# One list of work in two orders: linear attention with memory beside a dense layer, on one Trainium2 core

## The chip, the cores and the metric

The kernel runs on one core of one Trainium2 chip. A core has a matrix engine (PE in the profile, with PEld for its weight loads), a vector engine (DVE), a scalar engine (ACT), a general engine (POOL), a queue processor (SP) and 16 DMA engines. Each engine takes its own instructions strictly in order; engines meet only through semaphores. The metric is device time in microseconds of one execution; smaller is better. Time before: 229.43 us, the median of three runs (228.73 to 229.71).

## What is computed

One layer norm feeds two branches, and the input is added to their sum.

```python
def _A_ref(x, wq, wk, wv, wo, beta):          # S=2048, D=512, H=32 heads of 16, N=4 segments of L=512
    ...
    phi = lambda t: jnp.where(t > 0, t + 1.0, jnp.exp(t))
    g = _sigmoid(beta)
    for s in range(N):
        logits = jnp.einsum('bhqd,bhkd->bhqk', qs, ks) * scale + mask
        a_dot = jnp.einsum('bhqk,bhkd->bhqd', _softmax(logits), vs)
        a_mem = (phi(qs) @ M) / (phi(qs) . z + 1e-06)
        o = g * a_mem + (1.0 - g) * a_dot
        M, z = M + phi(ks)^T vs, z + sum(phi(ks))
    return o @ wo

def _B_ref(x, w1, w2):                        # F=1792
    return _silu(x @ w1) @ w2

xn = _layernorm(A_x)
return A_x + _A_ref(xn, ...) + _B_ref(xn, ...)
```

(The three lines on a_mem, M and z are shortened from einsums of the same meaning.)

## The kernel before

The work is cut into some 1,500 small pieces, each a Python function that issues the instructions of one piece on one engine. The string ORDER, a list written out by hand at the head of the file, names the pieces one after the other; the loop at the end of the kernel walks the list and calls each function. Nothing reorders the instructions after that, so the order of the words is the order on each engine. A word is a kind with numbers: `h0.10.2` is part 2 of block 10 of the first dense product of segment 0.

The kinds that matter here, with their lines:

- `S` (scores, lines 654 to 669): the scores of four heads go through PE into the tile psS, four banks of PSUM, of which there is one buffer; one ACT instruction (line 669) takes the exponential of all 2,048 columns into SBUF, and POOL masks the diagonal (677). There are 80 such pieces. The line of the list that begins with `S17` is called stage S17 below. The order of the 80 stages is the same in both lists.
- `E`, `O` (696): weights times values for the even and odd heads; `Ev`, `Ov`, `Oa` copy them out (v on DVE, a on ACT).
- `k`, `q`, `v`, `h` (322 or 324, in four parts or two): the dense products; `kv`, `qv`, `vv` copy a finished one out of PSUM on DVE, `ka`, `qa`, `va` do it on ACT (361, 371, 378). `ha` is the tanh of h on ACT (457), `hv` the rest of silu on DVE (462).
- `o`, `oc`, `od`, `oh`: the output product in whole, half or quarter width, 18 products of 512 columns for each of 16 row blocks; `st`, `sh` add the input and store (586, 633).
- `fa`, `ga` (395): the exponential of phi on ACT; `fp`, `gp` and `fv`, `gv` are its parts on POOL and DVE. `s`, `r`, `w`, `z`, `d`, `n`, `R`, `W`: sums, reciprocals, weights and their spreading over partitions by DMA.
- The layer norm: `xs` (or `xc`, `xd`) statistics on DVE, `xq` a square root on ACT (289), `xi` a reciprocal, `Nv` the normalised rows, `X` a transpose on PE with its copies `Xa`, `Xv` (743), `XD` a transpose by DMA (749). Rows 0 to 3 of the 16 use `xq`; later groups of four use `xg` on POOL.
- `tb` (295): one tiny exponential on ACT, whose only use is that the table of that function is loaded then. A first tiny square root (193) does the same for the square root at the start, before the list. The built program has a table load on ACT wherever the function changes between the square root and the others.
- `busy` (756): idle products of 128 columns on zeros. `lw0`, `lw1` (176): the loads of w2 and wo, issued from ACT's queue. `xl` (579): the load of a row block of the input, from SP.

A product counts as 512 columns. The four PSUM banks that psS leaves are shared by all other products (the pool `pp`, four buffers); a new product waits until the copy of an old one has run.

## Time and profile before

| | |
|---|---|
| median of the runs | 229.43 us (228.73 to 229.71) |
| span of the profiled execution | 227.4 us |
| what lies around the span, by the median | 2.0 us |
| PE busy | 217.2 us, 96% of the span |
| ACT busy | 198.0 us, 87% |
| DVE busy | 177.7 us, 78% |
| POOL busy | 113.9 us, 50% |
| 80 exponentials of the scores on ACT (669) | 150.2 us, 1,878 ns each |
| 56 tanh on ACT (457) | 32.8 us, 597 ns each (some overlap with what is ahead) |
| granted TensorE clock | 1.000 |

The page gives the time of the profiled execution's span alone; the 2.0 us is the median of the runs less that span. A busy PE is no PE at its peak: the ends of matmuls are modelled, and they overlap. What a stage costs is read from the starts of the exponentials in the timeline of ACT. From the first to the last of them, 12.72 to 206.62 us, there are 79 stages.

### The profile page before, as it was taken

What the parts mean: (1) busy time and instruction counts of PE and PEld (TensorE: products, weight loads), DVE (VectorE), ACT (ScalarE), POOL (GpSimd) and SP (SyncE); (2) the same over time, 40 slices, a digit from 0 to 9 for tenths busy, and PEclk for the clock granted to TensorE, in tenths of its full rate; (3) what the DMA queues carried; (4) which work ended last, traced back from release to release, by engine and by line L of the source; (5) the groups of instructions that cost most, each with busy time, mean ns of one, the idle gap of its engine ahead of it and who ended that gap; (6) DMA issues with size and microseconds to landing.
All of it is one profiled execution on the core that took longest, in us unless ns stands there. A gap on an engine that the chain in (4) does not pass through costs nothing.

```text
span 227.4 us, 7543 instructions
## 1 busy us (share of the span) xinstructions
PE 217.2 (96%) x3124; PEld 112.9 (50%) x3152; DVE 177.7 (78%) x351; ACT 198.0 (87%) x179; POOL 113.9 (50%) x173
## 2 busy tenths in 40 slices
...
ACT  3799998999999999999999899999999989897000
...
GB/s 181 361 381 68 77 52 299 60 55 57 61 22 158 72 35 47 96 15 112 41 40 113 75 53 58 35 117 42 22 100 66 88 36 84 29 63 130 29 90 94
DMA packets 34787, 20.55 MB, mean 90 GB/s; under 512 B 15680, under 2 KB 34240, under 8 KB 34752
## 3 DMA queue, kind: packets, MB, share of 16 engines
...
q8 instruction: 24, 0.39, 0.8%
...
HBM read 9.96 MB, written 2.10 MB: 53 GB/s over the span
## 4 chain that ended last, share of the span: by engine, by line
PE 62%; ACT 11%; DVE 11%; DMA 8%; issue 4%; SPq 2%; POOL 0%; DVEq 0%
PE ps L322 18%; PE psO L322 14%; PE psS L662 9%; ACT Pb L669 8%; PE ps L324 8%; PE psO L324 6%; PE psV L696 6%; DMA x_hi<-in_A_x_dram 4%; DMA spr<-rz 3%; ACT th L457 2%; DMA x_res<-in_A_x_dram 2%; DVE stats L272 1%; DVE o_out L586 1%; DVE kT L361 1%; PE psM L324 1%
## 5 line engine op out<-in xcount | busy, mean ns | idle before, releaser
L669 ACT ACTIVATE Pb<-psS 128x2048 bf16<-128x2048 f32 x80 | 150.2, 1878 | 5.8 <-PE psS L662 5.1
L677 POOL TENSOR_SCALAR_AFFINE_SELECT Pb<-Pb 128x512 bf16<-128x512 bf16 (+1 forms) x112 | 80.1, 729 | 85.1 <-ACT Pb L669 83.7
L462 DVE SCALAR_TENSOR_TENSOR hT<-th,ps 128x512 bf16<-128x512 bf16 x56 | 37.8, 679 | 14.1 <-ACT th L457 13.7
L322 PE MATMUL ps<-xnT,w_sb 128*128 128x512 bf16 (+1 forms) x177 | 43.3, 340 | 0.8 <-issue 0.5
L322 PE MATMUL psO<-w_sb,hT 128*128 128x512 bf16 (+2 forms) x139 | 36.1, 340 | 0.7 <-issue 0.5
L457 ACT ACTIVATE th<-ps 128x512 bf16<-128x512 f32 x56 | 32.8, 597 | 0.5 <-PE ps L322 0.4
L324 PE MATMUL psO<-w_sb,hT 128*32 128x128 bf16 (+2 forms) x468 | 26.7, 300 | 0.0
L322 PEld LDWEIGHTS <-w_sb 128*128 128x128 bf16 x184 | 17.1, 98 | 16.3 <-issue 3.3
L696 PE MATMUL psV<-Pb,Vz 128*32 128x128 bf16 (+3 forms) x512 | 23.1, 300 | 0.4 <-DVE oT L573 0.2
L322 PEld LDWEIGHTS <-hT 128*128 128x128 bf16 x149 | 13.6, 97 | 16.9 <-issue 4.8
L324 PE MATMUL ps<-xnT,w_sb 128*32 128x512 bf16 (+1 forms) x384 | 21.8, 329 | 0.0
L324 PEld LDWEIGHTS <-hT 128*32 128x32 bf16 x636 | 15.7, 97 | 9.7 <-issue 1.7
L696 PEld LDWEIGHTS <-Vz 128*32 128x32 bf16 x512 | 13.0, 96 | 10.6 <-issue 1.4
L662 PE MATMUL psS<-qT,kT 16*128 16x128 bf16 (+3 forms) x256 | 17.3, 301 | 0.9 <-ACT Pb L669 0.8
L662 PE MATMUL psS<-qT,kTo 32*128 32x384 bf16 (+3 forms) x256 | 17.2, 299 | 0.6 <-ACT Pb L669 0.2
L362 POOL TENSOR_SCALAR kTo<-kT,pm_odd 128x512 bf16<-128x512 bf16 x16 | 11.9, 747 | 8.2 <-DVE kT L361 7.3
L322 PE MATMUL ps<-xnT,wk_sb 128*128 128x512 bf16 (+1 forms) x66 | 15.4, 328 | 0.7 <-issue 0.5
L322 PE MATMUL ps<-wv_sb,xnT 128*128 128x512 bf16 x48 | 14.3, 380 | 0.6 <-issue 0.2
L662 PEld LDWEIGHTS <-kT 16*128 16x128 bf16 x256 | 5.9, 91 | 16.7 <-issue 16.2
L361 DVE CAST kT<-ps 128x512 bf16<-128x512 f32 x15 | 10.2, 687 | 4.6 <-PE ps L322 4.3
L586 DVE SCALAR_TENSOR_TENSOR o_out<-psO,x_res 128x512 bf16<-128x512 f32 x14 | 9.6, 687 | 5.3 <-PE psO L322 2.8
L719 DVE CAST oraw<-psV 128x512 bf16<-128x512 f32 x16 | 11.0, 688 | 3.4 <-PE psV L696 3.3
...
## 6 DMA issues: line engine op xcount, KB each, us to landing
...
```

The lines of the kernel that those rows point to most:

```text
L322: return [nc.tensor.matmul(out, lhsT=lhsT, rhs=rhs, start=start, stop=stop, skip_group_check=True)]
L324: nc.tensor.matmul(out[c : c + 32], lhsT=lhsT[:, c : c + 32], rhs=rhs, start=start, stop=stop, tile_position=(0, c), skip_group_check=True,)
L361: copy(out=kT[:, dt, :], in_=sts[s].pop(("k", dt))[:, :])
L362: nc.gpsimd.tensor_scalar(out=kTo[:, dt, :], in0=kT[:, dt, :], scalar1=pm_odd[:, 0:1], scalar2=1.0, op0=ALU.mult, op1=ALU.mult,)
L457: nc.scalar.activation(out=th[:], in_=sts[s]["h", ft][:, :], func=AF.Tanh, scale=0.5)
L462: nc.vector.scalar_tensor_tensor(out=st["hT"][:, ft, :], in0=st.pop(("th", ft))[:], scalar=1.0, in1=st.pop(("h", ft))[:, :], op0=ALU.add, ...
L586: out = nc.vector.scalar_tensor_tensor(out=o_out[:], in0=st.pop(("psO", j)), scalar=0.5, in1=st["x", j][:], op0=ALU.mult, op1=ALU.add)
L662: nc.tensor.matmul(psS[:, g, c0 : c0 + nq], lhsT=kk[rows, dt, kt * P : (kt + 1) * P], rhs=st["qT"][rows, dt, kt * P : L], start=True, stop ...
L669: exp = nc.scalar.activation(out=Pb[:, :, :], in_=psS[:, :, :], func=AF.Exp, scale=SCALE)
L677: mask = nc.gpsimd.affine_select(out=blocks, in_=blocks, compare_op=ALU.is_ge, fill=0.0, base=0, pattern=[[0, blocks.shape[1]], [1, P]], c ...
L696: nc.tensor.matmul(psV[32 * g : 32 * g + 32, kt * P : L], lhsT=Vzs[s % 2][:, kt, 4 * dt + g, par : par + 2, :].rearrange("p a d -> p (a d) ...
L719: copy(out=oraw[:], in_=sts[s].pop(("psV", 0))[:, :])
```

## The change

The string ORDER is replaced; nothing else is touched. The words are nearly the same set: each of the 80 stages stays where it was among the stages, and most other pieces move within their stage or to another. All differences of kind are these: `kv0.0` becomes `ka0.0` and `kv3.0` becomes `ka3.0` (from DVE to ACT), `qa0.1` becomes `qv0.1` and `ka3.3` becomes `kv3.3` (from ACT to DVE). The idle products are 44 and 6, as before, but all 50 stand ahead of the first transposes, where 44 stood. `tb` moves from behind the values' products to a place between the first square root of the start and the four of the layer norm. In the built program ACT then has four table loads where it had two: square root, exponential (295), square root (289), exponential (395, ahead of `fa0.0`). `lw0` moves from stage S4 to the prologue, behind the last of the four square roots.

The lists, cut to the parts that the text speaks of:

```diff
-kind odd ones0 ones1 zeros xc0 xd0 xc1 xq0 xi0 Nv0 busy44 xd1 xq1 xc2 xi1 X0.1 Nv1 xd2 Xa0.1 busy6 v0.0.0 v0.0.1 xq2 X1.1 Xa1.1 xs3 v0.0.2 v0.0.3 xq3 v0.1.0 xi2 v0.1.1 v0.1.2 v0.1.3 Nv2 xi3 X2.1 va0.0 k0.2.0 va0.1 Nv3 Xv2.1 X3.1 Xv3.1 k0.0.0 k0.0.1 k0.0.2 k0.0.3 q0.0.0 kv0.0 tb q0.0.1 q0.0.2 xs4 q0.0.3 qa0.0 k0.2.1 q0.3.0 fa0.0 q0.1.0
-S1 k0.2.2 xs6 q0.1.1 v0.3.0 v0.3.1 xs7 q0.3.1 q0.1.2 q0.1.3 xs5 xg4.4 q0.3.2 qa0.1 q0.3.3 fp0.0
-S2 k0.2.3 v0.3.2 qv0.3 v0.3.3 k0.1.0 kv0.2 fp0.2 fa0.2 k0.1.1 vv0.3 k0.1.2 k0.1.3 q0.2.0 q0.2.1
-S3 kv0.1 q0.2.2 h0.10.0 h0.10.1 Nv4 fv0.0 q0.2.3 h0.10.2 v0.2.0 h0.10.3 qv0.2 ha0.10 k0.3.0 k0.3.1
-S0 Nv5 v0.2.1 k0.3.2 hv0.10 h0.11.0 k0.3.3 h0.11.1 h0.11.2 kv0.3 h0.11.3 Nv7 xs8 XD5 ha0.11 h0.7.0
...
-S5 fv0.2 h0.5.0 v1.1.2 h0.5.1 hv0.1 v1.1.3 vv1.1 v1.3.0 h0.5.2 ha0.13 xs14 hv0.13 h0.5.3 ha0.5 t0.2 v1.3.1
...
-S4 qv1.1 k1.1.1 vv1.3 fv0.3 k1.0.0 k1.0.1 k1.0.2 lw0 h0.4.0 k1.1.2 Ev1 h0.4.1 k1.0.3 k1.1.3 kv1.1
...
-S14 fa1.1 h0.0.0 XD9 q1.3.2 q1.3.3 Nv8 h0.3.1 h0.3.2 hv1.11 E2
...
-S16 h1.9.1 h0.3.3 m0.0 h0.9.0 ha0.3 mv0.0 h1.9.2 h1.9.3 ha1.9 XD10 xl0.0 O2
...
-S64 k3.3.0 gp3.0 o1.3.17 oc1.3.10.0 st1.3 k3.3.1 h2.10.0 h2.10.1 ka3.3 ha2.10 sv2
...
-S74 o2.3.16 h3.12.0 st2.3 h3.12.1 ha3.12 h3.2.0 gv3.1 E14
-S73 h3.2.1 ha3.2 Ev14 oc2.2.5.1 o2.1.2 o2.2.16 o2.1.6 hv3.12 h3.8.0 o2.2.10 st2.2 hv3.2 o2.1.1 o2.1.5 h3.8.1 ha3.8 hv3.8
...
-S76 o2.1.8 d3.0 d3.1 h3.9.1 o2.1.9 oc2.1.10.1 h3.13.0 ha3.9 od2.1.12.0 oc2.1.11.1 h3.13.1 xl3.3 hv3.9 o3.0.12 od2.1.12.1 o2.1.4 o3.0.1 o2.1.13 ha3.13
...
+busy44 xc0 xd0 busy6 xs3 xc1 tb xd1 xq0 xi0 xq1 Nv0 X0.1 xi1 Nv1 xq3 xi3 Nv3 X1.1 Xa0.1 v0.0.0 Xa1.1 v0.0.1 X3.1 xc2 v0.1.0 v0.1.1 xd2 xq2 xi2 Nv2 v0.0.2 odd Xv3.1 lw0 v0.1.2 X2.1 Xv2.1 xs6 xs5 v0.0.3 k0.0.0 v0.1.3 ones0 va0.0 k0.0.1 k0.0.2 k0.0.3 va0.1 ka0.0 v0.3.0 q0.0.0 q0.0.1 fa0.0 q0.0.2 fp0.0 q0.0.3 qa0.0 xs4 q0.1.0 q0.1.1 q0.1.2
+S1 k0.2.0 k0.2.1 k0.2.2 k0.1.0 k0.1.1 k0.2.3 k0.1.2 kv0.2 k0.1.3 kv0.1 xs7 xg4.4
+S2 v0.3.1 v0.3.2 q0.3.0 q0.2.0 fa0.2 q0.3.1 q0.3.2 q0.1.3 fv0.0 q0.3.3 qv0.3 qv0.1
+S3 xs10 q0.2.1 q0.2.2 q0.2.3 ones1 qv0.2 h0.10.0 h0.10.1 h0.10.2 h0.10.3 ha0.10 v0.3.3 vv0.3 Nv6 XD6
+S0 h0.11.0 xs8 h0.11.1 h0.11.2 h0.11.3 Nv7 XD7 k0.3.0 k0.3.1 k0.3.2 k0.3.3 kv0.3 hv0.10 fp0.3 Nv5 XD5 Nv4 ha0.11 XD4 tanh
...
+S6 E0 hv0.11 Ev0 fa0.3 xs11 hv0.7 v1.3.0 v1.3.1 v1.3.2 v1.3.3 vv1.3 h0.1.0 h0.1.1
...
+S11 h0.0.3 ha0.0 fv0.1 t0.1 XD9 v1.2.0 v1.2.1 v1.2.2 v1.2.3 gate vv1.2 h0.6.0 h0.6.1 h0.6.2 h0.6.3 Nv8 XD8 ha0.6
+S14 v1.0.0 v1.0.1 v1.0.2 v1.0.3 h1.11.0 h1.11.1 hv0.6 vv1.0 h1.11.2 h1.11.3 ha1.11 E2 Ev2
...
+S16 hv1.9 xs14 h0.9.0 O2 Ov2 h0.3.1 h0.3.2 h0.3.3 ha0.3 m0.0 mv0.0 xs15 xs12 xg12.4
...
+S64 hv2.6 hv2.13 gp3.3 s2 sv2 r2.2 r2.1 xl2.2 fill h2.10.0 st1.3 h2.10.1 ha2.10 k3.3.0 k3.3.1 kv3.3 r2.3 hv2.10
...
+S74 h3.12.0 h3.12.1 hv3.5 ha3.12 E14 gp3.1 st2.3 Ev14 h3.2.0 h3.2.1 ha3.2 o2.2.16
+S73 hv3.12 o2.2.14 xl2.1 gv3.0 xl3.1 gv3.1 hv3.2 o2.1.8 h3.8.0 xl3.3 h3.8.1 ha3.8 o2.1.2 oc2.1.10.0 oc2.1.11.0 o2.1.3 od2.1.12.1
...
+S76 oc2.1.10.1 d3.1 h3.10.0 h3.10.1 R0.2 R0.1 hv3.6 R0.0 h3.11.0 ha3.10 hv3.10 d3.0 h3.11.1 ha3.11 o2.1.1 hv3.11 R0.3 o2.1.4 o2.1.17
...
```

The last stage, S78, holds all work behind the last scores. Its words are too many to show. It ends before with `st3.2 o3.1.17 oh17.1 st3.1 oh6.1 oh13.1 oh14.1 oh16.1 oh8.1 oh9.1 sh1`, and after with `o3.2.5 oh11.0 oh11.1 oh8.0 oh2.0 oh5.1 oh17.1 oh0.0 st3.2 oh15.0 oh5.0 sh1 oh13.0 sh0`. Counted in products of 512 columns, stage by stage (the scores themselves left out), the prologue has the same number in both; the stages whose count differs most, and S78, are:

| stage | S1 | S2 | S3 | S14 | S61 | S63 | S71 | S74 | S73 | S77 | S76 | S75 | S78 |
|---|---|---|---|---|---|---|---|---|---|---|---|---|---|
| before | 9 | 9 | 9 | 7.5 | 12 | 9 | 9.75 | 9.5 | 12.5 | 10.5 | 13.5 | 11 | 78 |
| after | 8 | 8 | 8 | 10.5 | 10.5 | 10 | 9 | 11.5 | 9.25 | 12 | 11.5 | 11.5 | 80.25 |

Stages with two ACT pieces beside the exponential are S5, S16, S64, S61, S73, S77 and S76 before, and S11, S61, S74, S77 and S76 after. (The tiny `tanh` of the gate, 0.20 us, is not counted.)

## The prediction

> **What bounds the kernel now.** The page's shares of busy time come first, and mislead: PE is busy for 96%, ACT for 87%.
>
> ```profile
> PE 217.2 (96%) x3124; PEld 112.9 (50%) x3152; DVE 177.7 (78%) x351; ACT 198.0 (87%) x179; POOL 113.9 (50%) x173
> ACT  3799998999999999999999899999999989897000
> ```
>
> The reader is to see that ACT is full from the third slice on and empty in the last three: it sets the pace until the scores are done, and PE alone works on the tail. How the pace arises is in the timeline of ACT:
>
> ```profile
> 116.21 1.88 ACT L669 ACTIVATE Pb<-psS 128x2048 bf16<-128x2048 f32 x1
> 117.98 0.59 ACT L457 ACTIVATE th<-ps 128x512 bf16<-128x512 f32 x1
> 118.59 1.88 ACT L669 ACTIVATE Pb<-psS 128x2048 bf16<-128x2048 f32 x1
> ...
> 123.35 1.88 ACT L669 ACTIVATE Pb<-psS 128x2048 bf16<-128x2048 f32 x1
> 125.75 1.88 ACT L669 ACTIVATE Pb<-psS 128x2048 bf16<-128x2048 f32 x1 [0.52 <-PE psS L662]
> ...
> 162.27 1.88 ACT L669 ACTIVATE Pb<-psS 128x2048 bf16<-128x2048 f32 x1
> 164.04 0.58 ACT L361 CAST kT<-ps 128x512 bf16<-128x512 f32 x1
> 164.51 0.61 ACT L457 ACTIVATE th<-ps 128x512 bf16<-128x512 f32 x1
> 165.00 1.90 ACT L669 ACTIVATE Pb<-psS 128x2048 bf16<-128x2048 f32 x1
> ```
>
> From one exponential to the next it is 2.38 us with one small piece between (116.21 to 118.59), 2.40 with none (psS has one buffer, so PE writes the next scores only when the exponential has read the last ones, 0.52 us), and 2.73 with two. A small piece is free, a second costs 0.35. Late in the kernel the stages are longer because PE has more products in them. Stages of 9.5 products last 2.49 (S55, S70), of 10.5 2.73 (S77), of 11 2.81 (S75), of 13.5 3.33 (S76): 0.2133 us a product (two take 0.43 in the chain of waits, whole or in four narrow parts) and 0.47 on top.
>
> **The prologue** comes third, since whatever delays the first exponential delays all 79 stages behind it. Again ACT's timeline:
>
> ```profile
> 1.72 1.28 ACT L193 ACT_TABLE_LOAD   x1 [1.72 <-PEq L818]
> 3.01 0.20 ACT L193 ACTIVATE spare<-zraw 128x1 f32<-128x1 bf16 x1
> 4.48 0.29 ACT L289 ACTIVATE rstd_all<-mv_all,eps 128x1 f32<-128x1 f32 x1 [1.27 <-DVE mv_all L275]
> ...
> 9.59 1.28 ACT L295 ACT_TABLE_LOAD   x1
> 10.88 0.20 ACT L295 ACTIVATE spare<-eps 128x1 f32<-128x1 f32 x1
> 11.63 0.59 ACT L371 CAST qT<-ps 128x512 bf16<-128x512 f32 x1 [0.55 <-PE ps L322]
> ...
> 12.72 1.88 ACT L669 ACTIVATE Pb<-psS 128x2048 bf16<-128x2048 f32 x1
> ```
>
> The first square root waits 1.27 us for the statistics; the second load ends 0.55 us before `qa0.0` has its product. So both loads are nearly covered now.
>
> **The change: table loads.** After, the load for `tb` follows the tiny square root at 3.2 and ends at 4.49, inside that wait; its tiny exponential ends at 4.69. But the square roots now need their table again: a third load, 4.69 to 5.97. The first root starts at 5.97, where it was 4.48. From there, with the rows of before: root 0.29; `xi0`, `Nv0` and their gaps 0.6, to 6.9; transposes from 7.1 (5.67 before). ACT copies the first half by 8.0, values from 8.05, `Xa1.1` ends at 8.9. The root of row 2 stands behind it and behind its statistics (`xc2`, `xd2` on DVE 8.1 to 9.0): 9.05 to 9.35; `Nv2` ends at 10.0, its transpose runs from 10.2, `Xv2.1` (0.42) ends at 11.15. PE then gives `v0.0.3` at 11.0, `v0.1.3` at 11.45 and `k0.0.3` at 12.1 (0.216 each and about 0.17 until ACT sees it). ACT, in order: `va0.0` 11.0, `va0.1` 11.55, `ka0.0` 12.1 to 12.7, the fourth load to 13.98, `fa0.0` to 14.6, `qa0.0` to 15.1, and the first exponential 0.5 behind it (12.22 to 12.72 before), at 15.6. That is +2.9 us. PE has nothing to put there: its last prologue product ends near 13.6, and S1's scores need `qa0.0`. The two ends: +2.3 if hand-overs are all as short as the shortest rows, and +3.5 if each of eight is 0.08 longer. I take +2.9.
>
> The Trainium skill, "ScalarE: Activation LUTs", section "What ACT_TABLE_LOAD costs", counts a drain of about 1.38 us behind each load of 1.28. Here the trace disagrees: the ACTIVATE at 3.01 starts where the load of 1.72 ends, and so does that at 10.88. By that section the two exposed loads would add some 2.8 us more and make it 234.7, an estimate.
>
> **Idle products.** Fifty stand ahead of the transposes instead of 44: none is added, six move. At 4.82/44 = 0.11 us they end at 6.5, before the first transpose can start at 7.1. They cost nothing while the third load covers them; were the transpose ready at 5.67, they would cost 0.8.
>
> **The load of w2** (`lw0`) comes 23 us earlier. The sixteen loads' 5.3 MB fill slices two and three at 361 and 381 GB/s and end near 17; w2 adds 1.8 MB from about 11 us. At 11.4 us 3.1 MB have moved and 2.2 are left of SP's: 1.2 of w1, 0.5 each of two groups of x. If the queues share evenly, at 0.185 MB/us each, w1 lands at 17.9, rows 8 to 11 at 20.6, the rest at 23.3. `h0.10` needs w1 at 20.9, and `xs10` on DVE, behind `qv0.1`, needs rows 8 to 11 at 21.2. Both are just met: nothing by this count, 2.1 us at worst if rows 8 to 11 come last. Its issue took 0.39 on ACT's queue; on SP's crowded queue the last issue took 3.93. ACT's ring then holds only two finished loads, so I take 0.39; the other end would move `va0.0` by 2.3 us.
>
> **The stages.** By the rule above. Second ACT pieces: S5, S16, S64 lose theirs, S11 gains one: -0.7. PE counts: S14 +0.34, S63 +0.20, S74 +0.42, S77 +0.30, S75 +0.11, S70 +0.06, five stages of 9.25 products +0.06 each; S73 (3.28 before) -0.84, S76 -0.41, S71 -0.17, S61, S55, S21 -0.05 each, S4 -0.07: together +0.1. Before has three stages that are long without a reason by the rule: S0 (2.68), S54 (2.81), S53 (2.59), 0.94 us over. Either the new order has none (-0.9) or as many of its own (0); I take half. Stages: -0.7 + 0.1 - 0.5 = -1.1, between -1.6 and -0.6.
>
> What moved between DVE and ACT (`ka0.0`, `ka3.0` against `qa0.1`, `ka3.3`) is in these counts. On POOL the memsets `ones1` (0.95) and `zeros` (0.57 for both) move from the prologue into S3 and S26, into its idle half; without that cover the masks of one stage would come 0.9 late, and `E` and `O` read them stages later.
>
> **The tail.** S78 has 2.25 more products, PE being dense there: +0.48. The last vector operations:
>
> ```profile
> 223.28 0.68 DVE L586 SCALAR_TENSOR_TENSOR o_out<-psO,x_res 128x512 bf16<-128x512 f32 x1
> 223.88 0.41 DVE L633 SCALAR_TENSOR_TENSOR o_half<-psS,x_res 128x256 bf16<-128x256 f32 x1
> 224.77 0.34 SPq L637 DMA_DIRECT2D out_dram<-o_half  x1
> ```
>
> Before, the last starts 0.2 after the last product (223.7) and its store waits 0.48 behind others. After, `st3.2`, `sh1`, `sh0` queue on DVE with only 1.5 products left: st3.2 starts 0.1 before the last product ends, then 0.6 and 0.4, so sh0 ends 1.2 behind it instead of 0.6 (+0.6), but its store finds SP nearly free (-0.4). The chain from `Oa15` over sums, reciprocals and spreads to `n3.3` has 39.5 products of cover (39.7 before): no stall. The last input rows (`xl3.0`, on SP behind the spreads) land some 15.4 us behind the scores of S78 (3.6 from issue, as before), `st3.0` wants them at 15.6. Tail +0.7, between +0.4 and +1.2.
>
> **Sum.** +2.9 - 1.1 + 0.7 = +2.5 on the span of 227.4: 229.9. With the 2.0 us that lie around it by the median, 231.9 us. The bounds of the terms alone give +1.1 to +4.1, so 230.5 to 233.5.
>
> **Rivals.**
> - *The early w2 load starves SP's.* For: the DMA engines are 9 tenths busy in slices two and three; DVE has `qv0.2`, `vv0.3`, `Nv6` and so the DMA transposes `XD6`, `XD7` queued behind `xs10`, and PE waits at `v1.3` in S6 for XD7, whose issue takes 1.24 to 2.5 us. Against: by even shares it is met by 0.6 us. Price: 1 to 2.5 us more, 233 to 234.5. Chance 0.13. The Trainium skill, "DMA: Bandwidth & Descriptors", section "Queues, rings and completion order", has each DMA engine alternate between the queues packet by packet; a late w2 then does take part of the rate from loads issued before it, which no row of before shows, and this rival's case follows.
> - *The new order has waits of its own* (a filler's product late in its stage, a bank not yet copied): five or more stages like S54 at 0.2 to 0.43, 1 to 2 us more, 233 to 234. Against: pieces late in a stage cost at most 0.1 before (S21, S55). Chance 0.15.
> - *Not slower: the added loads cost nothing on the path.* If ACT loads a table while it waits for its next operand, the roots start at 4.7 and `qa0.0` ends at 12.6: the first exponential at 13.1, +0.4. With stages at -1.6 and the tail at +0.4: 228.6; with the middle values 229.4. Decided by whether the first exponential starts before 13.8. Against: in both loads of before ACT starts nothing until the load ends. Chance 0.10.
> - *Something keeps ACT idle behind each exposed load.* Were each followed by as long a pause as the load itself, 1.28 us, the two would add 2.6: 234.5. Against: the two rows above. Chance 0.02. (This is the drain of the section named above.)
> - *The list does little* (order without effect): excluded by the two added loads in the program.
>
> **Chances.** The forecast has 0.60. The predicted time is its own, 231.9. The range takes its bounds and the slower rivals, and stops short of the not-slower one: 230.3 to 234.6. About 0.5% (1.15 us) is what a measurement of this kernel can tell from no change. The not-slower rival splits into 0.05 faster and 0.05 same; 0.03 of the forecast lies within 0.5%. Faster 0.05, same 0.08, slower 0.87.
>
> **What would show it.** Four ACT_TABLE_LOAD rows, the third ending near 6.0, the fourth between `ka0.0` and `fa0.0`; the first exponential at 15.6; 79 stages in 192.8 instead of 193.9; an end 21.5 us behind the last exponential's start (20.8 before). A first exponential before 13.8, or stages summing under 191, make it wrong.

## The result and the profile after

The change makes the kernel slower: 239.94 us, the median of five runs (238.28 to 240.72), against 228.88 us (228.09 to 229.71). The ratio is 1.0477, with a 95% interval of 1.043 to 1.0524. A second set of runs of the same kernel gave 240.24 us and 1.0536 (1.0476 to 1.0596). The forecast was 231.9 us, with 230.3 to 234.6 as its range: the sign was right, and the size was 11 us instead of 2.5. Medians in us are of all runs of a kernel, while the ratios leave out two runs that fell in a slower state of the chip, one of a_busy (242.40) and one of h_ba (234.66).

The busy shares and ACT's row of the 40 slices, from the page of after (span 236.6 us):

```profile
PE 220.5 (93%) x3152; PEld 114.0 (48%) x3152; DVE 179.2 (76%) x351; ACT 201.3 (85%) x181; POOL 115.1 (49%) x173
ACT  6589879999987899999999979999999999996000
```

No engine is busy for over 3.3 us more than before, and all shares are smaller: most of the 9.2 us of span is waiting. ACT's row shows eights and sevens in slices 5, 6, 12 to 14 and 24, where before it had nines. Its exponentials (669) waited 9.3 us for the scores, against 5.1 before. From the starts of the exponentials:

| | before | after | after, profiled again | forecast of the difference |
|---|---|---|---|---|
| first exponential starts | 12.72 | 15.33 | 15.19 | +2.9 |
| 79 stages | 193.90 | 198.73 | 200.86 | -1.1 |
| last one's start to the end of the span | 20.78 | 22.54 | 22.05 | +0.7 |
| span | 227.4 | 236.6 | 238.1 | +2.5 |

The first profile fell on the fastest of five executions (238.28); the second (239.77) is near the median, so its column is the better account of the 11 us.

The time of the start is as forecast. This is ACT's timeline of after (start, duration, engine, line, operation; in brackets the idle time before it):

```profile
3.31 1.28 ACT L295 ACT_TABLE_LOAD   x1
4.61 0.20 ACT L295 ACTIVATE spare<-eps 128x1 f32<-128x1 f32 x1
4.83 1.28 ACT L289 ACT_TABLE_LOAD   x1
6.12 0.29 ACT L289 ACTIVATE rstd_all<-mv_all,eps 128x1 f32<-128x1 f32 x1
...
12.44 1.28 ACT L395 ACT_TABLE_LOAD   x1
13.73 0.63 ACT L395 ACTIVATE ex<-kT 128x512 bf16<-128x512 bf16 x1
14.27 0.57 ACT L371 CAST qT<-ps 128x512 bf16<-128x512 f32 x1
15.33 1.88 ACT L669 ACTIVATE Pb<-psS 128x2048 bf16<-128x2048 f32 x1 [0.50 <-PE psS L662]
```

The third load ends at 6.1 and the fourth at 13.7, each followed at once by its function. The Trainium skill, "ScalarE: Activation LUTs", section "What ACT_TABLE_LOAD costs", adds a drain of about 1.38 us to each load; these rows show 0.02 us or less between a load and its function.

The stages are not as forecast. The largest excess is at S7 and S6. First PE's timeline of after, then DVE's:

```profile
26.23 1.03 PE L322 MATMUL ps<-xnT,w_sb 128*128 128x256 bf16 x8 [0.69 <-DVE kT L361]
...
29.48 0.29 PE L696 MATMUL psV<-Pb,Vz 128*32 128x256 bf16 x4 [1.12 <-DVE Vz L378]
```

```profile
22.94 1.52 DVE L301 TENSOR_SCALAR xn_t<-x_hi,mv_all,rstd_all 128x512 bf16<-128x512 bf16 x1
24.39 0.68 DVE L272 BATCH_NORM_STATS2 stats<-x_hi 128x6 f32<-128x512 bf16 x1
25.10 0.18 DVE L275 BATCH_NORM_AGGREGATE mv_all<-stats 128x2 f32<-128x6 f32 x1
25.20 0.38 DVE L301 TENSOR_SCALAR xn_t<-x_hi,mv_all,rstd_all 128x512 bf16<-128x512 bf16 x1
25.49 0.68 DVE L361 CAST kT<-ps 128x512 bf16<-128x512 f32 x1
26.09 0.68 DVE L462 SCALAR_TENSOR_TENSOR hT<-th,ps 128x512 bf16<-128x512 bf16 x1
26.69 1.11 DVE L301 TENSOR_SCALAR xn_t<-x_hi,mv_all,rstd_all 128x512 bf16<-128x512 bf16 x2
27.72 0.20 DVE L235 TENSOR_REDUCE kind<-ident 128x1 f32<-128x64 bf16 x1
...
28.75 0.67 DVE L378 CAST Vz<-ps 128x512 bf16<-128x512 f32 x1
```

DVE shows no idle time here; it works through a clump (a run of small operations queued one behind the other). The copy `kv0.3` (25.49), which frees a bank of PSUM for PE's next product, stands behind three layer-norm steps (`Nv6`, `xs8`, `Nv7`), and `vv0.2` (28.75), which `E0` needs, behind two more and the five operations of `kind`. `Nv6` (22.94) takes 1.52 us; `Nv7`, the same operation on the same shape, takes 0.38. The experiments come back to that. PE waits 0.69 and 1.12 us, the next scores are written late, and ACT's exponential waits. Later DVE does idle, on an item that needs a DMA. Its timeline at S20, then the rows of PE's timeline that wait for another engine, from S18 to S48:

```profile
73.14 0.55 DVE L486 TENSOR_SCALAR zsum<-zraw,evec 128x256 f32<-128x256 bf16 x1 [1.47 <-DMA zraw<-odd]
```

```profile
63.39 1.25 PE L322 MATMUL ps<-xnT,w_sb 128*128 128x256 bf16 x9 [0.54 <-DVE hT L462]
66.18 1.05 PE L324 MATMUL ps<-wv_sb,xnT 128*32 128x512 bf16 x16 [0.35 <-DVE hT L462]
75.28 0.59 PE L322 MATMUL ps<-xnT,w_sb 128*128 128x512 bf16 x2 [1.03 <-DVE kT L361]
77.50 0.61 PE L324 MATMUL ps<-xnT,wk_sb 128*32 128x512 bf16 x8 [0.86 <-DVE Vz L378]
105.05 0.29 PE L696 MATMUL psV<-Pb,Vz 128*32 128x256 bf16 x4 [0.38 <-POOL Pb L677]
136.13 0.73 PE L696 MATMUL psV<-Pb,Vz 128*32 128x512 bf16 x16 [0.27 <-DVE Vz L378]
137.49 1.05 PE L324 MATMUL ps<-xnT,wk_sb 128*32 128x512 bf16 x16 [0.63 <-DVE hT L462]
```

`sv0` (486) sat at the head of DVE's queue for 1.47 us waiting for the sums to be moved; the copies `kv2.1` and `vv2.1` stood behind it. With the two waits in S7 and S6, PE waited 5.5 us for operations of DVE in seven stages (S7, S6, S18, S22, S20, S24, S48), and 0.38 for a mask of POOL in S38. In before, PE's longest wait for DVE behind the prologue is 0.22 us.

In the tail, after's SP queue:

```profile
219.57 1.15 SPq L711 DMA_DIRECT2D zraw<-odd  x2
220.83 3.49 SPq L730 DMA_DIRECT2D oraw<-odd  x4
224.42 2.74 SPq L542 DMA_DIRECT2D spr<-rz  x4
...
233.65 0.87 SPq L637 DMA_DIRECT2D out_dram<-o_half  x2
```

The spread `d3.3` is among the four at 224.42. It needed only sums that had long been there, but stood in the list behind moves that wait for the last copies. The item that takes it on DVE (564) waited 2.08 us, and PE then 1.08.

### The profile page after: what moved, and what is told of

It reads as the page before. It is cut to its first block, busy times and chain, and to the rows that moved or that the text cites. A ratio compares the mean times of both kernels' runs of the same rounds, so it can differ in the third digit from the quotient of the medians.

```text
span 236.6 us, 7573 instructions
## 1 busy us (share of the span) xinstructions
PE 220.5 (93%) x3152; PEld 114.0 (48%) x3152; DVE 179.2 (76%) x351; ACT 201.3 (85%) x181; POOL 115.1 (49%) x173
## 3 DMA queue, kind: packets, MB, share of 16 engines
q10 hardware_dynamic: 2624, 2.62, 3.5%
## 4 chain that ended last, share of the span: by engine, by line
PE 35%; ACT 25%; DVE 19%; issue 7%; DMA 7%; SPq 3%; POOL 2%; DVEq 0%; ACTq 0%
ACT Pb L669 17%; PE ps L322 8%; PE psO L322 7%; PE ps L324 6%; PE psO L324 5%; PE psS L662 5%; ACT th L457 4%; PE psV L696 3%; ACT ex L395 3%; DMA zraw<-odd 2%; DVE stats L272 2%; DVE xn_t L301 2%; DVE hT L462 2%; DMA spr<-rz 2%; DMA x_lo<-in_A_x_dram 2%
## 5 line engine op out<-in xcount | busy, mean ns | idle before, releaser
L322 PE MATMUL ps<-xnT,w_sb 128*128 128x512 bf16 (+1 forms) x187 | 40.8, 340 | 2.3 <-DVE kT L361 1.7
L322 PE MATMUL psO<-w_sb,hT 128*128 128x512 bf16 (+2 forms) x154 | 34.0, 323 | 0.0
L324 PE MATMUL psO<-w_sb,hT 128*32 128x512 bf16 (+2 forms) x448 | 29.6, 325 | 0.0
L696 PE MATMUL psV<-Pb,Vz 128*32 128x384 bf16 (+3 forms) x512 | 23.4, 300 | 1.8 <-DVE Vz L378 1.4
L362 POOL TENSOR_SCALAR kTo<-kT,pm_odd 128x512 bf16<-128x512 bf16 x16 | 12.7, 795 | 17.4 <-ACT kT L361 9.6
L324 PE MATMUL ps<-xnT,w_sb 128*32 128x512 bf16 (+1 forms) x372 | 21.0, 332 | 0.0
L322 PE MATMUL ps<-xnT,wq_sb 128*128 128x512 bf16 (+1 forms) x68 | 13.4, 330 | 0.0
L554 DVE TENSOR_TENSOR oT<-spr,oraw 128x512 bf16<-128x512 bf16 x16 | 8.8, 552 | 6.0 <-DMA spr<-rz 5.9
L371 DVE CAST qT<-ps 128x512 bf16<-128x512 f32 x15 | 10.2, 685 | 3.9 <-PE ps L322 3.1
```

Source lines behind the costliest of these rows:

```text
L322: return [nc.tensor.matmul(out, lhsT=lhsT, rhs=rhs, start=start, stop=stop, skip_group_check=True)]
L324: nc.tensor.matmul(out[c : c + 32], lhsT=lhsT[:, c : c + 32], rhs=rhs, start=start, stop=stop, tile_position=(0, c), skip_group_check=True,)
L362: nc.gpsimd.tensor_scalar(out=kTo[:, dt, :], in0=kT[:, dt, :], scalar1=pm_odd[:, 0:1], scalar2=1.0, op0=ALU.mult, op1=ALU.mult,)
L371: copy(out=seg_tile(s, "qT")[:, dt, :], in_=sts[s].pop(("q", dt))[:, :])
L554: nc.vector.tensor_tensor(out=oT[:, dt, :], in0=sts[s].pop(("z", dt))[:], in1=sts[s]["oraw", dt][:], op=ALU.mult)
L696: nc.tensor.matmul(psV[32 * g : 32 * g + 32, kt * P : L], lhsT=Vzs[s % 2][:, kt, 4 * dt + g, par : par + 2, :].rearrange("p a d -> p (a d) ...
```

## The experiments

Theory: the loss is in DVE's order (clumps, and items that wait for a DMA, ahead of copies that PE needs) and goes with the words around it. Rivals: the early w2 load; the later start with its own timing; the clock. The diffs show changed words with their neighbours. Within each order the pieces are the same; only the number of idle products differs, in a_busy and the three called a_best. Stage lengths are those of one profiled execution each; how far they differ between executions is seen in S6, S18, S20 and S48 of kernels that have the same words there. The table has what their profiles show: starts of the exponentials, lengths of stages, the last exponential's start to the end. A label with `b_` changes before, one with `a_` changes after.

| kernel | first | S0 | S7 | S6 | S18 | S20 | S24 | S25 | S38 | S48 | S54 | tail | span |
|---|---|---|---|---|---|---|---|---|---|---|---|---|---|
| before | 12.72 | 2.68 | 2.40 | 2.37 | 2.38 | 2.38 | 2.38 | 2.38 | 2.39 | 2.39 | 2.81 | 20.78 | 227.4 |
| b_tb | 16.64 | 2.68 | 2.39 | 2.37 | 2.38 | 2.38 | 2.38 | 2.38 | 2.38 | 2.39 | 2.40 | 20.73 | 230.6 |
| b_lw | 15.12 | 2.66 | 2.40 | 2.37 | 2.38 | 2.38 | 2.38 | 2.38 | 2.38 | 2.39 | 2.40 | 21.22 | 229.6 |
| b_ones | 12.64 | 2.66 | 2.39 | 3.47 | 2.39 | 2.38 | 2.37 | 2.38 | 2.39 | 2.39 | 2.40 | 20.87 | 227.9 |
| h_ba | 12.41 | 2.55 | 2.40 | 2.37 | 2.39 | 2.38 | 2.37 | 2.37 | 3.04 | 2.55 | 2.41 | 21.55 | 228.6 |
| after | 15.33 | 2.38 | 3.03 | 3.59 | 2.98 | 3.36 | 3.27 | 2.38 | 2.96 | 3.66 | 2.40 | 22.54 | 236.6 |
| a_again | 15.19 | 2.37 | 3.04 | 5.31 | 2.57 | 3.30 | 3.27 | 2.44 | 3.01 | 3.17 | 2.39 | 22.05 | 238.1 |
| a_busy | 15.19 | 2.37 | 3.04 | 4.44 | 2.81 | 3.35 | 3.27 | 2.57 | 2.96 | 2.56 | 2.39 | 22.39 | 237.0 |
| h_ab | 15.19 | 2.38 | 3.03 | 4.40 | 2.56 | 2.82 | 3.27 | 2.44 | 3.01 | 2.39 | 2.91 | 21.42 | 239.3 |
| a_tb | 13.35 | 4.27 | 2.36 | 3.57 | 2.52 | 3.35 | 3.27 | 2.38 | 3.01 | 3.94 | 2.39 | 22.43 | 236.4 |
| a_tblw | 13.34 | 2.58 | 2.85 | 3.59 | 2.53 | 3.35 | 3.27 | 2.38 | 3.01 | 2.56 | 2.39 | 22.24 | 236.0 |
| a_s7 | 15.19 | 2.37 | 2.64 | 5.03 | 2.52 | 3.50 | 3.28 | 2.63 | 3.01 | 3.65 | 2.39 | 22.13 | 240.9 |
| a_s7lw | 15.19 | 2.37 | 2.63 | 4.53 | 2.62 | 3.36 | 3.27 | 2.60 | 3.01 | 3.53 | 2.39 | 22.06 | 237.8 |
| a_ones | 15.19 | 2.38 | 2.37 | 3.37 | 2.53 | 3.30 | 3.27 | 2.44 | 2.95 | 2.56 | 2.39 | 22.19 | 235.4 |
| a_v13 | 15.19 | 2.37 | 3.04 | 3.53 | 2.52 | 3.36 | 3.26 | 2.46 | 3.01 | 2.56 | 2.39 | 22.34 | 236.8 |
| a_sv | 15.19 | 2.38 | 3.03 | 4.33 | 2.52 | 2.38 | 3.02 | 4.09 | 2.96 | 3.89 | 2.39 | 22.50 | 238.3 |
| a_fix | 15.20 | 2.37 | 3.04 | 4.31 | 2.61 | 2.69 | 3.27 | 2.43 | 2.42 | 2.42 | 3.83 | 21.81 | 235.5 |
| a_best | 13.41 | 2.38 | 3.04 | 4.21 | 2.42 | 3.41 | 3.27 | 2.80 | 2.47 | 2.56 | 2.40 | 21.65 | 234.8 |
| a_best2 | 13.51 | 2.38 | 3.04 | 3.03 | 2.67 | 3.35 | 3.27 | 2.57 | 2.47 | 2.55 | 2.39 | 22.63 | 235.2 |
| a_best3 | 13.48 | 2.38 | 2.38 | 3.37 | 2.68 | 2.38 | 3.18 | 2.44 | 2.47 | 4.01 | 3.25 | 22.31 | 234.7 |

### The start: table loads and the w2 load

**a_tb**, after with `tb` behind the four square roots (two loads instead of four):

```diff
-xc1 tb xd1 xq0
+xc1 xd1 xq0
...
-xq2 xi2 Nv2
+xq2 tb xi2 Nv2
```

> The new order with the tiny exponential tb put behind the last of the four square roots: two table loads instead of four. If the two extra loads are what delays the start, the first exponential of the scores begins near 12.7 us instead of 15.33, every later stage keeps its length, and the span is 234.0 instead of 236.6. Rival (the start is bound by the layer norm's chain on DVE and the loads were hidden): it begins after 14.5 and the span stays above 235.7. Second rival (an early start brings S7 and S6 before their data, since DVE is the late one there): the start is 2.6 earlier, but S7 and S6 grow and less than 1.5 us is left at the end.

Measured: 237.81 us, ratio 1.0378 (1.0318 to 1.0437). The first exponential is 1.98 earlier and not 2.6: at 13.35 it is still 0.63 behind before's, so that part comes from the new order of the start and not from the loads. Stage S0 takes 4.27 instead of 2.38, and S7 begins at 24.75 (24.83 in after). DVE's timeline shows who held it:

```profile
21.29 0.69 DVE L272 BATCH_NORM_STATS2 stats<-x_hi 128x6 f32<-128x512 bf16 x1 [2.23 <-DMA x_hi<-in_A_x_dram]
```

The statistics `xs10` wait for input rows that land at 21.29. The prediction's w2 rival is in force here; in after the two loads' delay hides it, and `xs10` runs at 20.96 without a wait.

**a_tblw**, the same with the w2 load back in S4:

```diff
-Xv3.1 lw0 v0.1.2
+Xv3.1 v0.1.2
...
-S4 h0.4.2 h0.4.3
+S4 h0.4.2 lw0 h0.4.3
```

> The new order with two edits: tb behind the square roots (as in a_tb) and the load of w2 back in stage S4. With tb alone the first exponential came 2.0 us earlier, but S0 grew from 2.38 to 4.27: DVE waited 2.2 us for rows 8 to 11 of the input, and ACT 1.8 for beta. If it is the early load of w2 that keeps these late, S0 falls to 2.4, the first exponential is at 13.3, and the span is at most 234.5 (236.6 less 2.0). Rival (rows 8 to 11 land near 21 with or without w2): S0 stays above 3.8 and the span above 235.9.

Measured: 237.9 us, ratio 1.0402 (1.0351 to 1.0452). S0 takes 2.58, so the early w2 load is what delayed the rows. The span (236.0) misses the 234.5 that were expected. S6 stays at 3.59: its cause is another. Of the gain at the start little is left at the end, since S72 takes 5.15 (2.43 in after): DVE held there 1.59 by an item that waits for a spread, behind other moves on SP.

**b_tb**, before with the two added table loads, and **b_lw**, before with the early w2 load:

```diff
-kv0.0 tb q0.0.1
+kv0.0 q0.0.1
...
-xc1 xq0
+xc1 tb xq0
```

> The old order with tb put ahead of the first of the four square roots, so with four table loads. If the loads are the cause of the late start, the first exponential begins 2.6 to 3.0 us later than 12.72 and the span is 230.0 to 230.4 instead of 227.4, with the stages as they were. If the loads cost nothing on the path, the span stays within 0.5 of 227.4.

```diff
-k1.0.2 lw0 h0.4.0
+k1.0.2 h0.4.0
...
-xq3 v0.1.0
+xq3 lw0 v0.1.0
```

> The old order with the load of w2 put into the prologue, behind the last of the four square roots, as the new order has it. If this load alone delays SP's loads, rows 4 to 15 and the DMA transposes come later, and stages S1 to S6 grow by 1 us or more in sum. If the old order, which asks for rows 8 to 11 in S0 and after, has room, its stages stay within 0.2 us and the span within 0.5 of 227.4: then the loss takes both the early load and the early asking (xs10 in S3).

Measured: 232.16 us, ratio 1.0132 (1.0082 to 1.0181), and 230.47 us, ratio 1.0086 (1.0059 to 1.0113). The loads delay the old order's first exponential by 3.92, more than after's; the w2 load by 2.40, as PE waits 0.89 for wk. But no stage up to S48 grows in either: a later start alone makes none of after's long stages. In the windows of b_tb (stretch, its length, PE busy with instructions, granted clock, share of DMA, GB/s) the clock is part of the 3.92:

```profile
4.00:8.00 4.00, 2.04 (x30) 0.94 1.01 340
8.00:12.00 4.00, 4.00 (x23) 0.64 1.07 385
```

### Stages S7 and S6, and the clock

**a_s7**, after with `xs8`, `Nv4` and its transpose, and `kind` moved away from the copies:

```diff
-S0 h0.11.0 xs8 h0.11.1
+S0 h0.11.0 h0.11.1
...
-Nv5 XD5 Nv4 ha0.11 XD4 tanh
-S7 kind v0.2.0
+Nv5 XD5 ha0.11 tanh
+S7 v0.2.0
...
-Ev0 fa0.3
+Ev0 Nv4 XD4 fa0.3
...
-hv0.1 k1.2.0
+hv0.1 xs8 k1.2.0
...
-kv1.2 h0.13.0
+kv1.2 kind h0.13.0
```

> The new order with xs8, Nv4 and kind taken off DVE in stages S0 and S7 and put into S5, S6 and S9. If DVE's backlog is why S7 took 3.03 and S6 3.59 us (PE waited 0.69 for the copy kv0.3 and 1.12 for vv0.2), both fall to 2.38 to 2.5 and the span to about 234.8. Rival (the early load of w2 holds DVE's input or the DMA transposes back): S7 and S6 stay above 2.9.

**a_s7lw**, the same with the w2 load in S4:

> The new order with the DVE edit of a_s7 (xs8, Nv4 and kind out of S0 and S7) and the load of w2 back in S4. In a_s7 S7 fell to 2.64 but S6 grew to 5.03, where PE waited 2.18 for the DMA transpose of row block 7. If w2's load holds the transposes back, S7 and S6 are both below 2.7. Rival (three transposes in a row take this long whatever else is loaded): S6 stays above 3.5.

One execution each: 242.61 and 239.51 us. S7 falls to 2.64 and 2.63, as the theory of the clump has it. S6 rises to 5.03 and 4.53: PE now waits 2.18 (a_s7) for a transpose by DMA ahead of `v1.3`. The w2 load is not its cause, since S6 stays long without it. SP's row of a_again shows why transposes are late:

```profile
24.36 6.50 SPq L749 DMA_TRANSPOSE xnT<-xn_t  x4
```

Four of them, one after the other, take 6.5 us of SP's queue. Before had the same four from 20.94 on for 6.34, so that the queue was done at 27.3, and `v1.3` ran from 29.85 on; a_again starts it at 30.21, when the queue is not yet done (30.86).

**a_busy**, after with 16 idle products in the second group instead of 6:

```diff
-busy44 xc0 xd0 busy6
+busy44 xc0 xd0 busy16
```

> The kernel after with 16 idle products in the second group instead of 6: ten more, 1.1 us, into the 1.16 us in which PE stood idle before its first transposes (6.1 to 7.26). Theory: the executions of after differ (238.28 to 240.72) because the clock drops in that gap in some of them. Then the granted clock is 0.998 or more in every execution, the first exponential stays at 15.3 (15.2 to 15.6), and the median falls from 239.94 to about 238.3 (ratio 1.041, executions within 0.6 of each other). Rival: the clock is lost for another reason, the spread stays at 2 us and the median at 239.9 (ratio 1.048).

Measured: 240.61 us, ratio 1.0469 (1.0377 to 1.0561); granted clocks 1.000, 0.990, 0.993, 0.992. The theory that the clock is lost in PE's gap of the start falls.

**a_again**, after unchanged:

> The kernel after, unchanged, profiled once more. Theory that its executions differ by waits that hang on when transfers land: the stages that every kernel with after's early words shows (S7 3.0, S18 2.5 to 3.0, S22 2.7, S20 2.7 to 3.4, S24 3.3, S38 3.0) are long again, but S6 (3.59 once, 4.3 to 4.4 in three others), S48 (3.66 or 2.56) and S72 (2.43 or 3.21) may come out otherwise; the span differs from 236.6 by the sum of these within 0.5 plus the clock's part. Rival: all stages are as in the first profile within 0.1, and a longer execution is longer by the clock alone.

Measured: 240.24 us, ratio 1.0536 (1.0476 to 1.0596). S6 takes 5.31 and S5 3.00 (3.59 and 2.38 in the first profile). PE's waits and, below them, its windows in a_again:

```profile
29.34 0.29 PE L696 MATMUL psV<-Pb,Vz 128*32 128x256 bf16 x4 [1.12 <-DVE Vz L378]
30.21 1.37 PE L324 MATMUL ps<-wv_sb,xnT 128*32 128x512 bf16 x16 [0.58 <-DMA xnT<-xn_t]
```

```profile
28.00:30.00 2.00, 0.52 (x14) 1.00 0.44 66
30.00:31.00 1.00, 0.79 (x16) 0.90 0.13 24
31.00:34.00 3.00, 3.00 (x33) 0.50 0.19 37
34.00:36.00 2.00, 1.95 (x16) 0.95 0.00 0
```

And the same stretch in the first profile of after:

```profile
28.00:30.00 2.00, 0.88 (x24) 1.00 1.04 70
30.00:31.00 1.00, 1.00 (x28) 1.00 0.09 13
31.00:34.00 3.00, 3.00 (x30) 1.00 0.22 43
```

The wait for `vv0.2` is the same 1.12. A transpose that lands 0.58 too late leaves PE with 1.31 of 3 us busy instead of 1.88, and behind that the clock is halved for some 3.3 us. The same products and scores, from the start of `v1.3` to that of `h0.5`, take 4.63 us there (30.21 to 34.84) and 3.05 in the first profile (29.59 to 32.64). The late transpose alone does not bring this about: in the same 3 us PE was busy for 1.32 in a_sv, 1.25 in h_ab, 1.21 in a_busy and 1.34 in a_fix, with S6 at 4.3 to 4.4, and the clock stayed at 1.00 behind it. What decides is open. Half of 3.3 us is 0.7% of the span: a mean clock of 0.993. Of after's nine executions seven have 0.993 or less; of the 53 of before that stood beside the experiments none is under 0.995. Much of the 1.7 us between after's first profile and its median is read as this: S6 with a late transpose and a halved clock. Only this profile, and a_s7's at the same place (clock 0.50 from 32 to 34 us), show the place; for the other executions the mean alone is known.

**a_v13**, after with `v1.3` four products later, behind `h0.1`, and `kind` in S9:

```diff
-S7 kind v0.2.0
+S7 v0.2.0
...
-v1.3.0 v1.3.1 v1.3.2 v1.3.3 vv1.3 h0.1.0 h0.1.1
-S5 h0.1.2 h0.1.3 v1.1.0
+h0.1.0 h0.1.1 h0.1.2 h0.1.3 v1.3.0 v1.3.1
+S5 v1.3.2 v1.3.3 vv1.3 v1.1.0
...
-kv1.2 h0.13.0
+kv1.2 kind h0.13.0
```

> The kernel after with the product v1.3, which needs the transposes by DMA, six products later (behind h0.1), and the five small operations of kind in S9 instead of ahead of vv0.2. Theory: S6 is long for two reasons, vv0.2 late behind kind (1.12) and the transposes just landed or 0.66 late; without both S6 is 2.4 to 2.9 (3.59 to 4.44) and S7 as before the edit 3.0; the span falls by 0.8 to 1.9 and the executions lie closer together (median 238.0 to 239.0, ratio 1.040 to 1.044). Rival: v1.3's wait moves with it to S5 (3.0 or more) or the copies behind it come late at S9 and S4, and the median stays at 239.5 to 240.5 (ratio 1.047 to 1.050).

Measured: 238.87 us, ratio 1.045 (1.0412 to 1.0488), clocks 1.000, 1.000, 0.998, 0.993. The median falls by about 1 us as the theory has it, and one execution of four has a mean clock of 0.993 or less instead of seven of nine. But S6 is 3.53, over the expected 2.9: without the wait for `vv0.2` PE started `v1.3` at 30.26 all the same. The trace puts that wait (0.79) on DVE's statistics; the same start in a_again (30.21) and a_busy (30.30), where it is put on the transpose, speaks for the transpose. And S4 takes 2.89 (2.37), since `kind` now stands ahead of `hv0.13`: given back in part.

**a_ones**, after with one memset on POOL (`ones1`, 0.95 us) back at the head of the prologue, and **b_ones**, before with the same memset in S3:

```diff
-busy44 xc0
+ones1 busy44 xc0
...
-ones1 qv0.2
+qv0.2
```

```diff
-ones0 ones1 zeros
+ones0 zeros
...
-ha0.10 k0.3.0
+ha0.10 ones1 k0.3.0
```

> The kernel after with the memset ones1 back at the head of the prologue, where POOL idles from 2.90 to 12.5, instead of in S3. In after that memset runs on POOL from 23.37 to 24.32, and DVE's Nv6 (301) beside it takes 1.52 us from 22.94 to 24.46, where the same operation took 0.40 before. Theory: DVE is held by POOL's memset, and everything behind Nv6 is 1.1 late: kv0.3, vv0.2 and the transposes by DMA. Then Nv6 takes 0.4 to 0.8, kv0.3 runs by 24.8 instead of 25.49, S7 falls from 3.03 to 2.4 to 2.6, S6 from 3.6 to 5.3 to 2.4 to 3.0, no clock is halved there, and the median falls by 2 to 3 us to 237 to 238 (ratio 1.036 to 1.042). Rival: POOL's mask next to it holds Nv6 as long, or the clump alone makes the stages; S7 stays over 2.9 and S6 over 3.4, and the median at 239.5 or more.

> Before with one edit: ones1 in S3 instead of the prologue. Theory: the memset (0.95) runs on POOL about 19 to 21 us, beside DVE's parts of the layer norm and of phi (Nv4, fv0.0, Nv5), which take longer by up to 1 us there; S0 and S7 grow by 0 to 1 us together and the median lies between 228.4 and 229.8 (ratio 1.000 to 1.005). Rival: DVE's durations stay (0.63, 1.57, 0.85) and only POOL's later work moves; nothing changes by 0.1 us.

Measured: a_ones 237.34 us, ratio 1.037 (1.0332 to 1.0407), clocks 0.997 to 1.000; b_ones 229.86 us, ratio 1.0055 (1.0028 to 1.0083). This is POOL's timeline of after beside the 1.52 us of `Nv6`:

```profile
21.74 1.68 POOL L677 TENSOR_SCALAR_AFFINE_SELECT Pb<-Pb 128x1024 bf16<-128x1024 bf16 x2
23.37 0.95 POOL L781 MEMSET Vz<- 128x1024 bf16 x1
```

`Nv6` starts at 22.94 beside the masks and ends at 24.46, 0.14 behind the memset (24.32). Without the memset, DVE's timeline of a_ones has it at 0.59:

```profile
22.84 0.59 DVE L301 TENSOR_SCALAR xn_t<-x_hi,mv_all,rstd_all 128x512 bf16<-128x512 bf16 x1
23.35 0.68 DVE L272 BATCH_NORM_STATS2 stats<-x_hi 128x6 f32<-128x512 bf16 x1
24.06 0.18 DVE L275 BATCH_NORM_AGGREGATE mv_all<-stats 128x2 f32<-128x6 f32 x1
24.16 0.38 DVE L301 TENSOR_SCALAR xn_t<-x_hi,mv_all,rstd_all 128x512 bf16<-128x512 bf16 x1
24.46 0.69 DVE L361 CAST kT<-ps 128x512 bf16<-128x512 f32 x1
```

and the order before, given the memset, has in DVE's timeline of b_ones what after had:

```profile
21.93 1.21 DVE L301 TENSOR_SCALAR xn_t<-x_hi,mv_all,rstd_all 128x512 bf16<-128x512 bf16 x1
```

That was 0.40 at 22.02 before, although a mask of POOL (22.15 to 22.92) ran beside it there; the memset of b_ones (22.05 to 23.00) held it to its end. S7 falls from 3.03 to 2.37 in a_ones, and none of its four executions has a mean clock under 0.997. S6 stays at 3.37, more than expected: PE still waits 0.90 for `vv0.2` behind `kind`. In b_ones S6 rises from 2.37 to 3.47, more than the theory's bound of 1: DVE is 0.7 late by then, so its next `xn_t` (24.44) falls beside a mask of POOL (24.45 to 25.54) and takes 1.25 instead of 0.41, and PE waits 0.94 for `vv0.2` behind it. At the same time S54 and S53 lose their surplus, as in b_tb and b_lw. So one memset of 0.95 us, moved to where POOL had time for it, costs the new order some 2.6 us of its median, and the old one 1.0.

### The later waits

**a_sv**, after with `sv0` and the two reciprocals that follow it behind both copies; for this `vv2.1` moves up from S20, ahead of `r0.1`, `r0.3` and `w0` as well:

```diff
-hv1.8 sv0 r0.0 r0.2 k2.1.0
+hv1.8 k2.1.0
...
-kv2.1 lw1
+kv2.1 vv2.1 sv0 r0.0 r0.2 lw1
...
-o0.0.9 vv2.1 ha1.4
+o0.0.9 ha1.4
```

> The new order with the sums of segment 0 (sv0, r0.0, r0.2) moved on DVE from S21 to behind the copies kv2.1 and vv2.1 in S23. If DVE, held 1.47 us by sv0's wait for the DMA of the odd heads' sums, is what made PE wait for kv2.1 (1.03) and vv2.1 (0.86), S20 falls from 3.36 and S24 from 3.27 to 2.4, and the span to about 234.7. Rival (S20 and S24 are long because of the products or the weights' DMA there): they stay above 3.0, or the loss shows up again where the spread weights z are wanted, in S26 to S29.

One execution: 240.04 us. S20 falls to 2.38 (3.36), as it should if `sv0` is the cause; but with the same words up to there h_ab has 2.82 and a_fix 2.69, so one execution shows it only in part. S24 falls no further than 3.02 (3.27), where PE now waits 0.50 for a part of silu (462), and S25 rises to 4.09. DVE's timeline, then PE's:

```profile
82.09 0.56 DVE L554 TENSOR_TENSOR oT<-spr,oraw 128x512 bf16<-128x512 bf16 x1 [1.94 <-DMA spr<-rz]
```

```profile
83.30 0.40 PE L324 MATMUL ps<-xnT,w_sb 128*32 128x512 bf16 x4 [1.18 <-DVE hT L462]
```

The reciprocals and spreads that follow `sv0` are later too, so DVE waits 1.94 at `zv0.2`, and `hv1.10` stands behind that. The loss moved by three stages.

**a_fix**, three edits far from each other:

```diff
-E6 Ev6 oc0.1.10.0 h1.12.0 o0.3.17 gp1.3
+oc0.1.10.0 h1.12.0 o0.3.17 E6 Ev6 gp1.3
...
-dv1.1 hv2.8
+hv2.8 dv1.1
...
-o3.2.7 xl3.2 n3.2
+o3.2.7 d3.3 n3.2
...
-o3.1.6 d3.3 oh0.1
+o3.1.6 oh0.1
...
-W1 z3.3 od3.0.10.1
+W1 z3.3 xl3.2 od3.0.10.1
```

> The new order with three small moves at three places that do not touch each other. E6 three products later in S38 (PE waited 0.38 for a mask that POOL had queued behind a 1.20 copy): S38 falls from 2.96 to 2.4. On DVE hv2.8 ahead of dv1.1 in S44 (PE waited 0.63 for that bank behind the spread weights): S48 falls from 3.66 to below 3.0. In S78 the spread d3.3, which needs only old weights, ahead of the sums of the last odd heads on SP, and xl3.2 behind them (PE waited 1.1 for d3.3's product): the time from the last exponential's start to the end falls from 22.5 to 21.4 us. Rival (each is bound by the next thing in line): the places keep their length within 0.2. Note that stages before them may differ by what varies between executions; only these three lengths count.

One execution: 237.2 us. S38 falls to 2.42, so `E6` had waited there for POOL's mask. In the tail PE's wait of 1.08 for `d3.3` is gone, but two loads of input rows now stand together on SP at 226.06, and DVE waits 1.47 for such rows near the end: the tail is 21.81, against 22.54 and 22.05 in the two profiles of after. With the same edit a_best2 has 22.63 (DVE waits 2.02 for rows there). S48 falls to 2.42, but S54 takes 3.83, with DVE 2.89 behind a spread. S48 itself proved fickle: 3.66, 3.17 and 2.56 with the same words (after, a_again, a_busy), so this run tells little of it.

### Two halves

**h_ba**: before's list through S31 and after's from S32 on. **h_ab**: after's through S46 and before's from S41 on.

```diff
-S32 h1.6.0 v2.0.1 h1.6.1 h1.6.2 fa2.0 h1.12.0 o0.1.1 vv2.0 o0.1.15 h1.12.1 st0.1
+S32 o0.1.15 o0.3.6 o0.1.1 h1.6.0 od0.3.10.0 v2.0.1 vv2.0 o0.3.16 gv1.2 h1.6.1 h1.6.2 h1.6.3 o0.3.15 oc0.3.11.0 ha1.6
...
```

The lines are h_ba's first changed one; the stages behind it are after's, less what before's list has had by then. h_ab is the same the other way round.

> Before's list through stage S31, and after's from S32 on (the few pieces that only one of the two has had by then are moved over). Theory that each wait belongs to the words around it: the start and S7, S6, S18, S22, S20, S24 are as before, S38 2.96, S48 3.66 and the tail 22.5 as after. The span is then 236.6 less the 6.56 by which after's S32 began later: 230.0 (229.5 to 230.6), about 231.7 us, ratio 1.012. Rival, that the waits hang on when transfers and earlier pieces land: one or more of S38, S48 and the tail differs by over 0.4 from after's, and the span lies 1 us or more away.

> After's list through stage S46, and before's from S41 on (few pieces moved over likewise). Words theory: first exponential 15.3, S7 3.0, S6 3.6, S18 3.0, S22 2.7, S20 3.4, S24 3.3, S38 3.0 as after, then before's stages with S54 2.81 and S53 2.59 and before's tail of 20.8: span 227.4 plus the 7.13 by which after's S41 began later, 234.5 (233.8 to 235.5), with after's clock about 236.5 us, ratio 1.033. Rival, that the start's shift alone makes S54 and S53 lose their surplus, as in the two changed versions of before: both at 2.40, 0.6 less.

Measured: h_ba 231.72 us, ratio 1.0112 (1.0074 to 1.0151), and so within 0.001 of the ratio that was expected, but not stage by stage; h_ab 240.75 us, ratio 1.0499 (1.0401 to 1.0596), 4 us over. In h_ba the start and S7 to S25 are as before, and S38 is as in after. S48 (2.55 instead of 3.66) and the tail (21.55 instead of 22.5) are not, and the span of its profile, the fastest of ten executions, is 228.6 instead of 230.0: this is what its rival had named, so the ratio came out in part by luck. In h_ab the early stages are as in after, and S54 and S53 (2.91, 2.59) as before, so its rival fails. Both halves also have waits that neither list has: S32 2.97 in h_ba; S51 4.17 and S61 4.16 in h_ab. For S51, these are the rows of DVE and PE in h_ab:

```profile
143.03 0.43 DVE L554 TENSOR_TENSOR oT<-spr,oraw 128x512 bf16<-128x512 bf16 x1 [2.34 <-DMA spr<-rz]
```

```profile
144.11 0.38 PE L322 MATMUL ps<-phiQT,Mbf 128*128 128x512 bf16 x1 [1.63 <-DVE oT L573]
```

The clumps (S7, S6, S18, S22) and S38 go with the words around them, though not in size: h_ab has 4.40 at S6 and 2.56 at S18, after 3.59 and 2.98. The items that wait for a DMA cost what the moment costs: how long SP's queue is when the spread is issued, and whether a copy stands behind. A join of two lists makes new ones.

### Together

**a_best**: a_tblw's edits, a_busy's, `E6` and the tail of a_fix, and the layer norms of S16 to S18 behind the copies:

```diff
-mv0.0 xs15 xs12 xg12.4
+mv0.0 xs12
...
-S19 hv0.3 h0.9.1
-S18 Nv12 h0.12.0 h0.12.1 h0.12.2 Nv14 h0.12.3 ha0.12 hv0.9
+S19 hv0.3 xs15 xg12.4 h0.9.1
+S18 h0.12.0 h0.12.1 h0.12.2 h0.12.3 ha0.12 hv0.9 Nv12 Nv14
```

> The kernel after with the edits that helped or moved nothing: tb behind the square roots, the w2 load back in S4, ten more idle products, E6 three products later, the layer norms of xs15, Nv12, Nv14 behind hv0.3 and hv0.9, and in the tail the spread of the last denominators ahead of the load of input rows. If the waits are separate, the gains add: start -2.0, S38 -0.5, S18 and S22 -0.9, tail -0.7, span 232.5 (231.5 to 233.5) and, with the clock held, 234.2 us, ratio 1.023. Rival: what is saved comes back at the next item of DVE that waits for a transfer, as before at S25, S54 and S72; then the span is 234.5 to 236 and the ratio 1.032 to 1.038.

**a_best2**: that and a_v13's edit. **a_best3**: a_best and a_ones's edit.

> The best changed list so far (tb behind the roots, w2 load in S4, more idle products, E6, layer norms, tail) with the v1.3 and kind edit as well. S6 was 4.21 there. If S6's two causes are as said, it falls to 2.4 to 2.9 and the span from 234.8 to 233.0 to 233.6 (median 234.2 to 235.0, ratio 1.024). Rival, given back at S5, S9 or later: span 234.3 or more, ratio 1.029.

> The best changed list so far with ones1 at the head as well. There S7 was 3.04 and S6 4.21. By the theory both fall to 2.4 to 3.0, 1.2 to 2.4 us together, and the span from 234.8 to 232.4 to 233.6 (median 233.5 to 234.8, ratio 1.020 to 1.025). Rival: S7 and S6 stay, or later waits take it back, and the span is 234.3 or more.

Measured: a_best 235.85 us, ratio 1.0292 (1.0226 to 1.0358), clocks 0.997 to 1.000; a_best2 236.73 us, 1.035 (1.0307 to 1.0394); a_best3 236.27 us, 1.0307 (1.0264 to 1.0349). a_best gains some 4 us on after, and its expected gains of 4.1 us on the span become 1.8: S18 falls to 2.42 and S38 to 2.47, but S22 (3.27) and S27 (3.42, DVE 1.55 behind a spread) take it back. In a_best2 S6 falls from 4.21 to 3.03, and S4, S61 (3.63) and the tail (22.63) take that back. In a_best3 S7 and S6 fall by 1.5 together, and S20 by 1.0, but S48 (4.01), S54 (3.25) and S61 (4.22) rise, with DVE 2.0 behind a spread at each of the first two. The medians of both lie above a_best's, so the memset's price is not a sum that can be taken off any list. None of the versions run is faster than before.

## Why the prediction was wrong

- *Table loads:* the four loads stood where they were put, and the time of the start came out, +2.61 and +2.47 for +2.9. But the working gave all of it to the loads, and a_tb gives them 1.98: 1.28 for the fourth load, and 0.7 for the third, since without it the second root waits 1.26 for DVE and the first copy of the transposes still starts at 6.99 (7.70 in after, 6.19 before). The other 0.63 is the new order of the start, so the closeness is in part luck. The first root started at 6.12 (5.97). The rival "not slower" is out (15.3 against its bound of 13.8), and so is the one of an idle ACT behind each load. The idle products cost nothing, as argued: with ten more (a_busy) the start is at 15.19 again.
- *The load of w2:* "nothing by this count" was right for after, and the rival's mechanism was real: a_tb and a_tblw show rows landing at 21.29 instead of 20.08. It was hidden by the table loads, which were priced separately; the two do not add.
- *The stages:* this step failed. For the counted terms the rule held (S11 +0.34, S64 -0.33, S74 +0.42, S73 -0.84, S77 +0.30, S76 -0.41 as forecast; S14 not, +0.03 instead of +0.34), and before's surplus at S0, S54, S53 did vanish (-0.91). But the sum was -1.1, and the stages gave +4.8 and +7.0. The sentence that failed is "Either the new order has none (-0.9) or as many of its own (0); I take half". It took the waits that one list shows as a measure for the other, and the rule counts only PE's products and ACT's pieces. DVE's queue in the new list was not walked piece by piece; eight stages (S7, S6, S18, S22, S20, S24, S38, S48) show +6.5 together in the first profile, and PE's waits there are on DVE in all but S38, where it is a mask of POOL. The surplus went the forecast way in part by luck: S54 and S53 also lose it in b_tb, b_lw and b_ones, which have before's words there.
- *The memset:* this step failed too. It said that `ones1` moves "into its idle half", and that without that cover masks would come 0.9 late. POOL did have the time; DVE did not, as its `Nv6` beside the memset took 1.52 us. a_ones shows the price. The trace of before had a hint: the same `xn_t` took 0.85 beside POOL pieces (at 20.06) and 0.41 with POOL idle (at 23.73).
- *The rival "The new order has waits of its own"* names what happened, at chance 0.15. It was priced at 1 to 2 us from the small waits of before, whose order was free of such things; its "against", that late pieces cost at most 0.1, spoke of PE's fillers and not of DVE.
- *The tail:* +0.7 forecast, +1.8 and +1.3 measured. The sentence "no stall" failed: the cover of 39.5 products was counted, but not that `d3.3` is queued on SP behind moves that wait; PE waited 1.08 for it. What that is worth at the end stays open: the same edit gives 21.81 in a_fix and 22.63 in a_best2.
- *The clock* was no part of the sum. In S6 a late piece costs twice: by the wait, and in some executions by a halved clock behind it.
- *Small terms:* what lies around the span was taken as 2.0 us; in after it is 1.7 (238.28 less 236.6). The loads that fill before's first slices are thirteen in its timeline and not sixteen; their 5.3 MB, on which the count rests, fit the rates of the first three slices.

What stays open: which way the 6.5 us divide among the waits one by one, since each edit moved others, and no version run wins back more than some 4 us of the 11 (a_best); why the same words gave S48 3.66, 3.17 and 2.56, and S20 2.69 to 3.36; what decides whether the clock is halved; and how much of after's median each landing makes up, since only two of its nine executions are known stage by stage.
